# Retention attention and an ELU block on one core: no tensor operation on GpSimd, the decay of the state merged into its sum, one written plan for all steps

## The chip, the cores and the metric

The kernel runs on one core of one Trainium2 chip. The metric is the device time in microseconds of one execution, the median of several runs. The core has five engines with an instruction stream of their own: TensorE (PE, matmuls; PEld are its weight loads), VectorE (DVE), ScalarE (ACT), GpSimd (POOL) and SyncE (SP). Each runs its instructions in order and waits for others by semaphores. SP, ACT and POOL also issue DMAs.

## The reference

The inputs are `q`, `k`, `v` of shape (4, 8, 768, 64): 4 batches, 8 heads, 768 positions, 64 columns; a decay `lam` per head; and two weight matrices, 512 x 2048 and 2048 x 512. Attention goes through each sequence in 12 blocks of 64 positions and carries a 64 x 64 state per head:

```python
for b in range(nb):
    intra = (qb @ kb.T * Dmask) @ vb              # Dmask: lam ** (i - j) for i >= j, else 0
    inter = (qb * lam_pow) @ kv_state             # lam_pow: lam ** (i + 1)
    out[:, :, sl] = intra + inter
    kv_state = lam ** 64 * kv_state + (kb * rev_pow).T @ vb
h = x @ w_in                                      # x: out, as 3072 tokens x 512
g = where(h > 0, h, exp(min(h, 0)) - 1)
return g @ w_out
```

## The kernel before

The work is cut into 24 **steps**. A step is one block of 64 positions of two batches with all heads, 128 tokens; even steps belong to batches 0 and 1, odd ones to 2 and 3, so step s continues the state of step s - 2. Two steps make a **group** of 256 tokens for the ELU block. There are 12 groups.

Attention of a step s, with the names that the plan's words use:

- Loads (`lk`, `lq`, `lv`; line 79): keys, queries and values by GpSimd's DMA queue, cast to 16 bits on the way, twelve buffers each. `w` loads half a quarter of w_in into `wi` (line 100), `y` a quarter of w_out into `wo` (line 111). Step 0's keys and queries come raw by SP and ACT and are cast by `Fk`, `Fq` (line 181).
- Transposes of keys and queries: for s < 10 on TensorE, copied out of PSUM by `C` (`att_C`, lines 239 to 245); from step 10 on by DMA on SP's queue (`T`, `dma_T`, line 256), into two buffers.
- A visit `Aso.us.ss.sx` of TensorE (`visit`) does, for four steps at once: the products of keys and queries of step ss (line 352), the new state product of step us (line 344), the two output products of step so (328 with the old state and the decayed queries, 337 with the masked scores and the values), and the transposes of step sx. `I` begins the first of the output products ahead.
- `P` masks the scores (line 228), `V` decays the values (`vd`, line 193), `Q` decays the queries (`qs`, line 220, two buffers), `D` and `d` decay the old state (`sd`, line 211 on VectorE or GpSimd, line 206 on ScalarE), `N` adds it to the new product in PSUM and writes the state (line 281; for the first two steps a copy, line 285), `X` copies the output to `xt`, the block's input (line 269).

The ELU block: `H` and `h` are units of matmuls with w_in (line 428, 1024 result columns of 128 rows in 8 or 16 matmuls) into one of two PSUM buffers `psH`. `E` and `e` compute exp and relu on ScalarE (lines 438 and 440, or 472 and 474 for the later groups), `G` and `g` join them on VectorE (line 445 or 475). In the first form PSUM is free once ScalarE has read it, in the second when `g` is done. The first six steps go through w_out by `M` (line 495), the output copied by `Z` (502). From group 3 on the product with w_out is done in Strassen's manner, by seven products `p` of eight matmuls each (line 551) over half-size sums `s` (line 533, of `g`) and `B` (line 521, of the weights); `k` keeps a part of PSUM in SBUF (line 581), `a` and `c` add parts to the output tile (lines 585 and 589, four output buffers), `o` stores it (line 570). `K` are constants.

The order of each engine's instructions is the order in which the program emits them. For the first groups it is written out as a string of words, `start`; its beginning is

```python
"Fq K0 Fk V0 A...0 C0 A.0.. K1 A..0. P0 A...1 N0 C1 A0... X0 V1 A..1. P1 A.1.. A1... X1 "
"N1 D2 H0.0.1.0 D3 E0.0.1.0 A...2 V2 C2 Q2 H0.1.1.0 A.2.2. I2 R P2 E0.1.1.0 A2... "
"G0.0.1.0 H0.0.2.4 X2 N2 H1.0.1.0 E0.0.2.4 D4 G0.1.1.0 A...3 G0.0.2.4 E1.0.1.0 C3 V3 "
"H1.0.1.4 Q3 E1.0.1.4 H0.0.2.6 A.3.3. I3 P3 G1.0.1.0 E0.0.2.6 H0.0.2.10 A3... E0.0.2.10 "
```

The early loads are emitted ahead of it: v0, k1, q1, v1, both halves of w0, k2, q2, v2, both halves of w1, k3, q3, v3; `R` emits the later ones. From group 3 on a loop over groups and their eight units `u` emits the rest. Each group there has eight units, eight joins, seven products, four sums, and two of each attention step. In it `decay_q` is on GpSimd for steps 12 and 14 and from 15 to 23, and on VectorE else; `decay_s` is on VectorE up to step 10, on ScalarE for 11 to 13, on GpSimd from 14 to 21.

Of the kernel before, what the change touches and what calls it, by code (L numbers as in the profile page):

```python
# [16 lines left out]
def kernel(  # L17
# [41 lines left out]

    NB = 12  # L60
# [23 lines left out]
    def load_step(s):  # L84
        load("k", s)
        load("q", s)
        load("v", s)

# [8 lines left out]
    def load_wi(i, halves=range(2)):  # L97

        for c in halves:
            ins = nc.gpsimd.dma_start(  # L100
                out=wi[i][half(c)],
                in_=moe_w_in[c * DM // 2 : (c + 1) * DM // 2, i * WB : (i + 1) * WB].rearrange(
                    "(g p) f -> p g f", p=64
                ),
            )
            if (i, c) == (2, 1):

                ins.wait_op(crossed, 1, "sem-ge")

    def load_wo(i):  # L110
        nc.gpsimd.dma_start(
            out=wo[i][:],
            in_=moe_w_out[i * WB : (i + 1) * WB, :].rearrange("(g p) f -> p g f", p=128),
        )

# [14 lines left out]
    load("v", 0)  # L130
    load_step(1)
    load_wi(0)
    load_step(2)
    load_wi(1)
    load_step(3)
    load_wi(2, [0])

# [95 lines left out]
    def att_C(s):  # L233
        if s >= NT:
            return
        T = asb.tile([128, 2, NHP, 2, L], FP16, tag="T", bufs=4, name=f"T{s}")
        psT = st[s].pop("psT")
        if s < NQ:
            nc.vector.tensor_copy(T[:, 0].rearrange("p j r t -> p (j r t)"), psT[0])
            nc.scalar.copy(  # L240
                out=T[:, 1].rearrange("p j r (t g) -> p (j r t) g", g=8),
                in_=psT[1].rearrange("p (g x) -> p x g", g=8),
            )
        else:
            nc.vector.tensor_copy(
                T[:].rearrange("p i j r t -> p r (i j) t"),
                psT.rearrange("p r (x t) -> p r x t", t=L),
            )
        st[s]["T"] = T
# [12 lines left out]
    def att_X(s, eng):  # L262
# [5 lines left out]
        if eng is nc.scalar:  # L268
            nc.scalar.copy(out=to, in_=O)
        else:  # L270
            eng.tensor_copy(to, O)

    def att_N(s):
# [6 lines left out]
        if c:  # L280
            nc.vector.tensor_tensor(
                out=to, in0=psU, in1=st[s]["sd"][:].rearrange("p y j d -> p y (j d)"), op=ALU.add
            )
        else:
            nc.vector.tensor_copy(to, psU)
# [149 lines left out]
    def mm1_e(grp, c0, nc_, n0):  # L435
# [4 lines left out]
        nc.scalar.activation(r[:], psH[:], AF.Relu)  # L440
# [22 lines left out]
    def elu(grp, u):  # L463

        psH, nb, T, name = unit[grp, 0, 2, u]
        if grp == 3 or grp == 4 and u < 6:
            mm1_e(grp, 0, 2, u)
            mm1_g(grp, 0, 2, u, NF2)
            return

        r = msb.tile([128, nb, T], FP32, tag="r", bufs=4, name=f"r{name}")
        nc.scalar.activation(r[:], psH[:], AF.Relu, scale=-1.0)  # L472
        e = msb.tile([128, nb, T], FP32, tag="e", bufs=4, name=f"e{name}")
        nc.scalar.activation(e[:], r[:], AF.Exp, scale=-1.0)  # L474
# [6 lines left out]
    nacc = [0]  # L481
# [8 lines left out]
    def mm2(s, n0):  # L490
        if n0 == 0:
            acc[s] = M[nacc[0] % 2][:]
            nacc[0] += 1
# [6 lines left out]
    def mm2_o(s):  # L500
        o = msb.tile([128, DM], FP32, tag="o", bufs=4, name=f"o{s}")
        nc.scalar.copy(out=o[:], in_=acc.pop(s))
# [56 lines left out]
    def part(grp, i):  # L559
        d = res.setdefault(grp, dict(A=M[0], B=M[1]))  # L560
        lo, hi = slice(0, HD), slice(HD, DM)
# [6 lines left out]
    def store(s, o, cols, queues=(nc.sync, nc.sync)):  # L568
        for r in range(2):
            queues[r].dma_start(out=rows(s, r)[:, cols], in_=o[half(r), cols])  # L570
# [7 lines left out]
    def keep(grp, tag, src, bufs=2):  # L578

        t = res[grp][tag] = msb.tile([128, *src.shape[1:]], FP32, tag=tag, bufs=bufs, name=f"{tag}_{grp}")  # L580
        nc.scalar.copy(out=t[:], in_=src)
# [5 lines left out]
    def c2(grp, queues=(nc.sync, nc.sync)):  # L587
# [5 lines left out]
        store(2 * grp + 1, d[1], slice(0, DM), queues)  # L593
# [12 lines left out]
    def later_loads():  # L606
        load_wi(2, [1])
        load_wo(0)
        load_wi(3)
        load_wo(1)  # L610
        load_wo(2)
        load("k", 4)
        load("q", 4)
        load_wo(3)
        load("v", 4)
        load_step(5)
        load_step(6)
        load_step(7)
        load_step(8)
        load("k", 9)  # L620
        load("q", 9)
        load("k", 10)
        load("q", 10)
        load("v", 9)
        load("k", 11)
        load("q", 11)
        load("v", 10)

    start = (
# [14 lines left out]
    )  # L646
    steps = {
        "I": lambda s: visit(s, None, None, None, True), "C": att_C, "P": att_P, "X": lambda s: att_X(s, nc.scalar),
        "Y": lambda s: att_X(s, nc.vector), "N": att_N, "D": lambda s: decay_s(s, eng=nc.vector), "L": load_step,
        "V": lambda s: decay_v(s, nc.vector if s < 99 else nc.gpsimd),  # L650
        "Q": lambda s: decay_q(s, nc.vector if s < 10 else nc.gpsimd),
        "H": mm1_h, "E": mm1_e, "G": mm1_g, "M": mm2, "Z": mm2_o, "K": consts, "B": w_sum, "T": dma_T,
    }
    for word in start.split():
        if word[0] == "A":
            visit(*(int(x) if x else None for x in word[1:].split(".")))
        elif word[0] == "R":
            later_loads()
        elif word[0] == "F":
            cast0(word[1])  # L660
        else:
            steps[word[0]](*(int(x) for x in word[1:].split(".") if x))

    lo, hi = slice(0, HD), slice(HD, DM)

    five = [(3, 2), (3, 4), (3, 6), (4, 0)]
    nload = 12
    for grp in range(3, NG):  # L670
        old, new = grp - 2, grp - 1
        for u in range(8):
            mm1_h(grp, 0, 2, u, NF2)
            s = 2 * grp + 2 + u // 4
            if s < NS and u % 4 == 0:

                if nload < NS:
                    load("k", nload)
                    load("q", nload)
                if nload <= NS:  # L680
                    load("v", nload - 1)
                    nload += 1
            if s < NS and u % 4 == 1:
                if s not in (10, 12):
                    decay_q(s + 1, nc.vector if s < 10 else nc.gpsimd)
                if s not in (10, 11, 12):
                    decay_s(s + 1, eng=nc.vector if s < 10 else nc.gpsimd)
                visit(
                    s, s if s < NS - NPR else None, s + 1 if s + 1 < NS else None,
                    s + 2 if s + 2 < NT else None,  # L690
                )
                dma_T(s + 3)

            if (grp, u) in five:
                mm2(5, 4 * five.index((grp, u)))
            end = grp == NG - 1
            if old >= 3 and u in (0, 2):
                part(old, {0: 3, 2: 7}[u])
            if new >= 3:
                at_u = {1: 2, 3: 4, 4: 1, 5: 5, 6: 6, 7: 3} if end else {3: 2, 4: 1, 5: 4, 6: 5, 7: 6}  # L700
                if u in at_u:
                    part(new, at_u[u])

            if old >= 3 and u == 1:
                add(old, 0, hi, res[old]["A"][:, hi], "p35")
                store(2 * old, res[old][0], slice(0, DM), ((nc.gpsimd if end else nc.sync),) * 2)
            if old >= 3 and u == 0:
                g_sum(old, 3)
            if new >= 3 and u in (4, 5, 6):
# [101 lines left out]
```

## Time and profile before

| | before |
|---|---|
| median of 3 runs | 205.23 us (204.94 to 205.42) |
| span of the profiled execution | 204.2 us |
| TensorE busy | 189.6 us, 93% |
| VectorE busy | 168.7 us, 83% |
| ScalarE busy | 146.5 us, 72% |
| GpSimd busy | 123.4 us, 60% (with its DMA issues) |

The profiled execution's own time outside the profiler is not listed; its span lies 1.03 us below the median. The span runs from the first to the last instruction. Groups in the profile read: line, engine, operation, written tile, read tiles, partitions x elements, count, then busy time and mean duration, then idle time before them and what ended it.

### The profile page before, as it was taken

The numbers are of one execution on the slowest core, as the hardware profiler recorded it, in microseconds if no ns is written. First come the engines' busy times: TensorE is split into PE (matmuls) and PEld (weight loads), VectorE is DVE, ScalarE is ACT, GpSimd is POOL, SyncE is SP. The second block draws the span as 40 slices with busy tenths as digits, with TensorE's granted clock in tenths as the row PEclk, the third lists the DMA queues.
The fourth block names the chain that finished last, engine by engine and source line by source line (L and its number), as shares of the span: only waits on it lengthen the run. The fifth ranks groups of instructions, "written<-read, shape, count | busy, mean of one in ns | idle before, by whom it ended". The sixth has DMA issues, their size and how long they took to land.

```text
span 204.2 us, 7590 instructions
## 1 busy us (share of the span) xinstructions
PE 189.6 (93%) x3216; PEld 156.6 (77%) x3216; DVE 168.7 (83%) x279; ACT 146.5 (72%) x283; POOL 123.4 (60%) x174
## 2 busy tenths in 40 slices
PE   0679899999999999999999989999999999999991
PEld 0457777647777777888888878888888888888881
DVE  4776996489989998999989999989979866758672
ACT  5626987635774879999878677788688788876820
POOL 8977832598998959997709999999222200020000
PEclk9999999999999999999999999999999999999998
DMA  6999999999999999999999999999915404004043
GB/s 102 157 171 171 152 206 196 180 124 156 117 148 150 173 108 172 153 134 78 74 163 109 206 105 86 185 111 105 169 27 69 94 0 108 0 6 100 3 103 103
DMA packets 94194, 24.36 MB, mean 119 GB/s; under 512 B 86160, under 2 KB 91152, under 8 KB 94160
## 3 DMA queue, kind: packets, MB, share of 16 engines
q0 software_dynamic: 73744, 13.64, 94.7%
q1 hardware_dynamic: 19968, 9.77, 26.9%
q10 hardware_dynamic: 448, 0.46, 1.0%
q8 instruction: 25, 0.41, 0.9%
q14 instruction: 9, 0.07, 0.1%
HBM read 27.27 MB, written 6.29 MB: 164 GB/s over the span
## 4 chain that ended last, share of the span: by engine, by line
PE 85%; DVE 4%; DMA 3%; POOL 3%; issue 2%; ACT 1%; POOLq 0%; DVEq 0%
PE psH L428 40%; PE psM L551 23%; PE psM L495 10%; DMA wi<-in_moe_w_in_dram 3%; PE psO_None L328 2%; POOL vn L79 1%; PE psZ L352 1%; PE psO_None L337 1%; PE psHB L551 1%; PE psHA L551 1%; DVE s L533 1%; PE psZ L344 1%; DVE g L475 1%; POOL kn L79 1%; PE psO L359 1%
## 5 line engine op out<-in xcount | busy, mean ns | idle before, releaser
L428 PE MATMUL psH<-xt,wi 128*128 128x256 f16 (+1 forms) x896 | 100.1, 261 | 1.9 <-ACT e L438 0.6
L428 PEld LDWEIGHTS <-wi 128*128 128x128 f16 x896 | 78.2, 100 | 13.3 <-issue 2.1
L475 DVE SCALAR_TENSOR_TENSOR g<-e,psH 128x512 f16<-128x512 f32 x58 | 39.6, 683 | 14.3 <-ACT e L474 13.8
L472 ACT ACTIVATE r<-psH 128x512 f32<-128x512 f32 x58 | 34.7, 598 | 18.3 <-PE psH L428 18.2
L474 ACT ACTIVATE e<-r 128x512 f32<-128x512 f32 x58 | 36.5, 630 | 1.8
L79 POOL DMA_DIRECT2D kn<-in_k_dram x46 | 32.2, 720 | 9.2 <-DMA wo<-in_moe_w_out_dram 5.1
L79 POOL DMA_DIRECT2D vn<-in_v_dram x48 | 34.1, 741 | 2.0 <-DMA wi<-in_moe_w_in_dram 1.1
L438 ACT ACTIVATE e<-psH 128x512 f32<-128x512 f32 x38 | 22.8, 601 | 14.7 <-PE psH L428 14.4
L551 PEld LDWEIGHTS <-s 128*128 128x128 f16 x288 | 28.1, 98 | 3.3
L445 DVE SCALAR_TENSOR_TENSOR g<-e,r 128x512 f16<-128x512 f32 x38 | 25.7, 685 | 4.1 <-ACT r L440 4.0
L220 POOL TENSOR_TENSOR qs<-TD,powi 128x512 f16<-128x512 f16 x11 | 13.9, 1264 | 19.3 <-PE psO_None L328 13.1
L79 POOL DMA_DIRECT2D qn<-in_q_dram x36 | 25.3, 735 | 0.0
L551 PE MATMUL psM<-wt,s 128*128 128x256 f16 x192 | 24.9, 273 | 0.0
L495 PE MATMUL psM<-wo,g 128*128 128x512 f16 x96 | 24.0, 379 | 0.0
L440 ACT ACTIVATE r<-psH 128x512 f16<-128x512 f32 x38 | 22.9, 602 | 0.0
L551 PEld LDWEIGHTS <-g 128*128 128x128 f16 x216 | 20.6, 98 | 2.6
L193 DVE TENSOR_TENSOR vd<-vn,rev 128x512 f16<-128x512 f16 x22 | 17.2, 783 | 1.8 <-DMA vn<-in_v_dram 1.7
L228 DVE TENSOR_TENSOR P<-psZ,mask 128x512 f16<-128x512 f32 x24 | 16.4, 684 | 2.0 <-PE psZ L344 1.1
L551 PE MATMUL psM<-wo,g 128*128 128x256 f16 x136 | 17.6, 272 | 0.0
L495 PEld LDWEIGHTS <-g 128*128 128x128 f16 x96 | 8.7, 98 | 7.0
L570 POOL DMA_DIRECT2D out_dram<-o x2 | 1.1, 574 | 21.1 <-DVE o L585 21.1
L533 DVE TENSOR_TENSOR s<-g 128x1024 f16<-128x1024 f16 x18 | 13.8, 764 | 0.0
(85 smaller groups left out, 228.7 us busy)
## 6 DMA issues: line engine op xcount, KB each, us to landing
out_dram<-o SPq DMA_DIRECT2D x43, 128.0 KB, 3.3
vn<-in_v_dram POOLq DMA_DIRECT2D x48, 64.0 KB, 5.0
kn<-in_k_dram POOLq DMA_DIRECT2D x46, 64.0 KB, 4.3
qn<-in_q_dram POOLq DMA_DIRECT2D x36, 64.0 KB, 4.5
wi<-in_moe_w_in_dram POOLq DMA_DIRECT2D x8, 256.0 KB, 8.9
wo<-in_moe_w_out_dram POOLq DMA_DIRECT2D x4, 512.0 KB, 12.6
qn<-in_q_dram POOLq DMA_DIRECT2D x5, 128.0 KB, 5.3
kraw<-in_k_dram SPq DMA_DIRECT2D x2, 128.0 KB, 4.7
```

The lines of the kernel that those rows point to most:

```text
L79: nc.gpsimd.dma_start(out=keep[s][half(r)], in_=src[b + r, :, c * L : (c + 1) * L, :].rearrange("h p d -> p h d"),)
L193: eng.tensor_tensor(out=st[s]["vd"][:], in0=vn[s][:], in1=rev[:].unsqueeze(2).broadcast_to([128, H, D]), op=ALU.mult,)
L228: nc.vector.tensor_tensor(out=d["P"][:].rearrange("p y j t -> p y (j t)"), in0=psS, in1=mask[:].rearrange("p y j t -> p y (j t)"), op=ALU. ...
L428: nc.tensor.matmul(psH[:, i, :], lhsT=wi[n // 4][:, kk, (n % 4) * 128 : (n % 4 + 1) * 128], rhs=xt[grp][:, kk, c0 * 128 : c0 * 128 + T], s ...
L438: nc.scalar.activation(e[:], psH[:], AF.Exp)
L440: nc.scalar.activation(r[:], psH[:], AF.Relu)
L445: nc.vector.scalar_tensor_tensor(out=place(grp, c0, nc_, n0, nb, step), in0=e[:], scalar=-1.0, in1=r[:], op0=ALU.add, op1=ALU.min,)
L472: nc.scalar.activation(r[:], psH[:], AF.Relu, scale=-1.0)
L474: nc.scalar.activation(e[:], r[:], AF.Exp, scale=-1.0)
L475: nc.vector.scalar_tensor_tensor(out=place(grp, 0, 2, u, 2, NF2), in0=e[:], scalar=-1.0, in1=psH[:], op0=ALU.add, op1=ALU.max,)
L495: nc.tensor.matmul(acc[s], lhsT=g_of(s, n), rhs=wo[n // 4][:, n % 4, :], start=(n == 0), stop=(n == NFT - 1),)
L551: nc.tensor.matmul(to, lhsT=lhsT, rhs=rhs, start=start and n == 0, stop=stop and n == NF2 - 1, skip_group_check=True,)
```

## The change

- GpSimd only issues loads and one store. All `Q` are on VectorE.
- `D` and `d` are not used. For steps 2 to 21 `N` is four `scalar_tensor_tensor` instructions, one for each pair of heads, that multiply the old state by its decay and add the new product in PSUM.
- A trailing `.1` on a word moves an operation between ScalarE and VectorE: the relu of `E` and `e`, the copies of `X`, `Z` and `k` go to VectorE, those of `C` to ScalarE (its second digit sends the queries' copy to VectorE).
- One string, `plan`, orders everything from the first load to the last store; the loop is gone. The store order on SP changes with it, and step 18 is stored by GpSimd's queue, as before.
- The wait of the second half of w2 on a semaphore of TensorE goes. The PSUM banks of the first six steps' products are assigned by a tuple.

```diff
+    plan = (
+        "lk1 K1 lq1 K0 Fq Fk lv0 lv1 A...0 C0 A..0. P0 A...1 C1.1.1 A..1. P1 A1... lk2 lq2 w1.1 "
+        "V0 w1.0 A0... lv2 lk3 X1.1 A.0.. w0.1 lq3 w0.0 V1 A...2 C2.1 X0.1 w2.1 lv3 lq4 lk4 w2.0 "
+        "H0.0.2.4 V2 N0 A.1.. N1 H0.0.2.6 A.2.2. w3.0 E0.0.2.6 Q2 I2 A...3 P2 A2... E0.0.2.4.1 "
+        "y0 G0.0.2.4 C3.1.1 Q3 w3.1 H0.0.1.0 E0.0.1.0.1 X2 G0.0.2.6 H1.0.1.0 H0.1.1.0 N2 V3 "
+        "A.3.3. E0.1.1.0 P3 I3 A3... lq5 lk5 y1 y2 G0.0.1.0 E1.0.1.0.1 H1.0.1.8 X3.1 H1.1.1.8 "
...
+        "T14 N10 Z4 h4.0 e4.2 k3.p2 X10 lq16 lv16 lk16 h4.5 P11 p3.1 lk15 lq15 T15 h4.6 e4.0 "
+        "g4.2 V11 s3.4 e4.5 s3.3 A11.11.12. h4.3 g4.5 Q12 e4.6 T16 lv15 p3.4 g4.6 e4.3 g4.0 N11 "
+        "X11 h4.7 e4.7 p3.5 h5.1 g4.3 a3.1 g4.1 p3.6 h5.0 g4.7 P12 A12.12.13. V13 V14 k3.c45 "
+        "e5.1 p3.3 e5.0 X12 k3.p35 h5.2 e5.2 g5.1 p4.2 Q13 g5.0 a3.0 o6.0 p3.7 h5.3 N12 g5.2 P13 "
...
+        "e11.3 s10.2 s10.4 g11.2 c9 p10.1 g11.3 h11.5 e11.4 s10.3 p10.5 g11.4 h11.6 e11.5.1 "
+        "a10.1 e11.6 p10.6 k10.u2 g11.5 k10.c45.1 h11.7 p10.3 p10.7 g11.6 a10.2 e11.7 g11.7 j "
+        "p11.1 s11.1 s11.2 k11.u1 s11.4 c10 o20.0 o17.0 o19.0 o21.0 p11.4 p11.5 p11.6 k11.c45 "
+        "k11.u2 s11.3 p11.2 a11.3 o22.1 p11.7 c11 o23.3 p11.3 a11.2 o22.2 o18.5 "
+    )
...
-        if c:
+        if c and "sd" not in st[s]:
+            for j in range(NHP):
+                nc.vector.scalar_tensor_tensor(
+                    out=state[s][:, :, j, :], in0=state[s - NPR][:, :, j, :], scalar=lamL[:, j : j + 1],
+                    in1=psU[:, :, j * D : (j + 1) * D], op0=ALU.mult, op1=ALU.add,
+                )
+        elif c:
...
-        nc.scalar.activation(r[:], psH[:], AF.Relu)
+        if on_dve:
+            nc.vector.tensor_scalar_max(r[:], psH[:], 0.0)
+        else:
+            nc.scalar.activation(r[:], psH[:], AF.Relu)
...
+        "Q": lambda s, e=0: decay_q(s, by(e)), "H": mm1_h, "E": mm1_e, "G": mm1_g, "M": mm2, "Z": mm2_o,
```

`by(0)` is VectorE; no `Q` or `V` of the plan has the digit that would name GpSimd. Of the plan the beginning, the steps 10 to 13 and the end are shown; between them it goes on in the same way.

More of the change, by code (lines that the diff above doesn't have):

```diff
@@ L95, with load_wi @@
     crossed = tc.alloc_semaphore("crossed")
[L97 to L108, printed above, removed]
+    def load_wi(i, c):
+        nc.gpsimd.dma_start(
+            out=wi[i][half(c)],
+            in_=moe_w_in[c * DM // 2 : (c + 1) * DM // 2, i * WB : (i + 1) * WB].rearrange(
+                "(g p) f -> p g f", p=64
+            ),
+        )
     def load_wo(i):
@@ L267, in att_X @@
         O = st[s].pop("O").rearrange("p r (y t) -> p r y t", y=NHP)
[L268 to L271, printed above, removed]
+        copy(eng, to, O)
     def att_N(s):
@@ L498, in mm2, with mm2_o @@
             )
-    def mm2_o(s):
+    def mm2_o(s, on_dve=0):
         o = msb.tile([128, DM], FP32, tag="o", bufs=4, name=f"o{s}")
-        nc.scalar.copy(out=o[:], in_=acc.pop(s))
+        copy(nc.vector if on_dve else nc.scalar, o[:], acc.pop(s))
         for r in range(2):
@@ L631, with sums @@
-    start = (
[14 rows of a table removed]
-    )
-    steps = {
[L648 to L652, printed above, removed]
+    def sums(grp, i):
+        d = res[grp]
+        if i == 0:
+            add(grp, 0, hi, d["A"][:, hi], "p35")
+        if i == 1:
+            add(grp, 0, lo, d["A"][:, hi], "p2")
+        if i == 2:
+            add(grp, 0, hi, d["B"][:, hi], "u2")
+        if i == 3:
+            add(grp, 0, lo, M[1][:, lo], "u1")
```

248 lines of the change are left out of this document (75 added, 173 removed), and 50 rows, old and new, of tables (plan, start).

## The prediction

> **What bounds the kernel now.** I read the page first, then the waits of TensorE, the chain that ended last, and the busy time of the engines by stage.
>
> ```profile
> span 204.2 us, 7590 instructions
> ...
> PE 189.6 (93%) x3216; PEld 156.6 (77%) x3216; DVE 168.7 (83%) x279; ACT 146.5 (72%) x283; POOL 123.4 (60%) x174
> ...
> PE 85%; DVE 4%; DMA 3%; POOL 3%; issue 2%; ACT 1%; POOLq 0%; DVEq 0%
> ```
>
> TensorE is busy for 189.6 of 204.2 us and makes 85% of the chain. A busy TensorE could still be one that waits inside its matmuls, so the next views ask where it stood still and how fast it ran.
>
> ```profile
> PE psM L398 <- DVE qn L181: 6.5, 1, 6.5
> PE psZ L344 <- DVE P L228: 0.8, 1, 0.8
> PE psH L428 <- ACT e L438: 0.6, 1, 0.6
> PE psH L428 <- DVE g L475: 0.5, 2, 0.3
> ```
> ```profile
> 13.24 1.89 PE psH L428 x16
> ...
> 82.63 0.87 PE psH L428 x8
> 83.51 0.87 PE psM L551 x8
> ...
> 199.24 0.89 PE psHB L551 x8
> ```
>
> Its first instruction waits 6.5 us for the first queries; the other named waits are 0.8 us or less, and the two on VectorE's `g` are 0.5 us together. From then on the chain is one unit of eight matmuls (128x256) behind another, 0.87 us each, until 200.1 us; the last 4 us are the last sum and its stores. Both kernels issue the same matmuls. So the change can only win in the first 25 us, in the small waits behind them, and in the tail; it can lose wherever another engine falls behind.
>
> ```profile
> 79.90:160.30 80.40, 79.87 (x1354) 69.63 (x1354) 74.78 (x117) 66.26 (x127) 58.88 (x74) 1.00 1.43 121
> 110.00:130.00 20.00, 19.47 (x292) 16.84 (x289) 19.67 (x28) 15.15 (x28) 20.00 (x25) 1.00 1.56 140
> ```
>
> Columns: stretch, length, busy time of TensorE, its weight loads, VectorE, ScalarE, GpSimd; clock; DMA. From step 10's visit to step 21's, VectorE is busy 74.78 of 80.40 us (93.0%), and TensorE loses 0.53 us. All 0.53 us are lost in the 20 us where VectorE reaches 98.4%. VectorE is the second bound, and where it fills up, TensorE waits.
>
> **What leaves GpSimd, and what that gives VectorE.**
>
> ```profile
> L220 POOL TENSOR_TENSOR qs<-TD,powi 128x512 f16<-128x512 f16 x11 | 13.9, 1264 | 19.3 <-PE psO_None L328 13.1
> L211 POOL TENSOR_TENSOR sd<-st,lamL 128x512 f32<-128x512 f16 x8 | 9.4, 1174 | 2.3 <-DVE st L281 2.3
> ...
> 119.87 1.23 POOL L220 TENSOR_TENSOR qs<-TD,powi 128x512 f16<-128x512 f16 x1
> 120.08 1.58 DVE L193 TENSOR_TENSOR vd<-vn,rev 128x512 f16<-128x512 f16 x1
> ```
> ```profile
> L193 DVE TENSOR_TENSOR vd<-vn,rev 128x512 f16<-128x512 f16 x8 | 5.5, 685 | 1.8 <-DMA vn<-in_v_dram 1.7
> ...
> L193 DVE TENSOR_TENSOR vd<-vn,rev 128x512 f16<-128x512 f16 x11 | 9.7, 882 | 0.0
> L533 DVE TENSOR_TENSOR s<-g 128x1024 f16<-128x1024 f16 x11 | 9.0, 815 | 0.0
> L533 DVE TENSOR_TENSOR s<-s,g 128x1024 f16<-128x1024 f16 x6 | 4.9, 820 | 0.0
> L533 DVE TENSOR_TENSOR s<-g,s 128x1024 f16<-128x1024 f16 x5 | 4.1, 829 | 0.0
> ```
>
> Nineteen operations leave GpSimd, 23.3 us. While one of them runs, VectorE's operations with two inputs in SBUF stretch: `vd` takes 685 ns in the first 60 us, where GpSimd computes nothing, and 882 ns on average in the stretch above, 1.58 us in the case shown. With 685 ns as the clean time of both groups, the stretch holds 11 x 0.20 = 2.2 us for `vd` and 22 x 0.14 = 3.0 us for `s`: 5.2 us that VectorE gets back. GpSimd itself keeps only loads and one store; no wait of TensorE ends on it, so nothing else is earned there.
>
> **What VectorE gets.**
>
> ```profile
> L281 DVE TENSOR_TENSOR st<-psZ,sd 128x512 f16<-128x512 f32 x20 | 13.6, 681 | 0.0
> L585 DVE TENSOR_TENSOR o<-psM,p 128x256 f32<-128x256 f32 x15 | 6.3, 418 | 0.4
> L589 DVE TENSOR_TENSOR o<-psM,c 128x512 f32<-128x512 f32 x8 | 5.5, 690 | 1.2 <-PE psM L551 1.2
> ...
> 24.90 1.28 DVE L445 SCALAR_TENSOR_TENSOR g<-e,r 128x512 f16<-128x512 f32 x2
> ```
>
> Two 0.68 us operations back to back take 1.28 us, so each costs VectorE about 0.61 us. The merged sum of a step is four instructions of 128 columns in place of one of 512. No row shows that size: 256 columns take 418 ns and 512 take 690, which continues to about 0.28 us for 128. Less the 0.07 us overlap this is 0.2 us a piece; I take 0.9 us a step, between 0.8 (full overlap) and 1.14 (none), 0.28 more than the 0.61 of before; the upper end of all is 418 ns a piece, as if nothing were saved by the smaller size. The Trainium skill ("VectorE: DVE Perf Modes", the section on the fixed extra latency) speaks against such splitting: an instruction pays a fixed cost whatever its size, and small tiles pay it per tile; its section on the DRAIN adds that the next operation does not start before the pipe is empty, so that the count should be kept low. By that a step costs four whole durations, and my sum would be 1 us higher. The pair at 24.90 shows some overlap; no row shows it for small operations.
>
> In the stretch from A10 to A21 the plan has 42 `h` and 36 `p` units, against 44 and 37 now: 3 x 0.873 = 2.6 us less TensorE work, so 77.8 us. VectorE there: 74.78, less 5.2 of contention; three more full operations (nine more decayed queries, three sums `s`, two `g` and one `c` fewer), +1.9; eleven merged sums at +0.28, +3.1; one more small copy, +0.4. That is 74.9 of 77.8 us, 96.3%; with 1.14 us a sum it is 99.6%. So the contention that goes pays for about what comes, per time VectorE is fuller than now. Between the two rows of the window view (93.0% loses 0.66% of the time, 98.4% loses 2.65%) 96.3% reads as 1.9%, or 1.5 us in place of 0.5: **+0.9 us**. A decayed query now stands in VectorE's order and holds up all behind it if its transposes are late.
>
> ```profile
> 85.68 1.20 SPq L256 DMA_TRANSPOSE TD<-kn  x1
> 86.97 2.15 SPq L256 DMA_TRANSPOSE TD<-qn  x1
> ...
> TD<-qn SPq DMA_TRANSPOSE x14, 5.3
> ```
>
> The second transpose of a pair is issued 1.3 us after the first and lands 5.3 us later, 6.6 us in all. In the plan each query from step 12 on has at least 9.9 us of TensorE work between what frees the buffer of its transposes and itself. So this costs nothing; a transpose over 3 us late would show on every engine.
>
> Outside the stretch VectorE also takes relus and copies from ScalarE (eight relus, four casts of `xt`, seven kept parts, two output copies), gives ScalarE six copies of transposes, and drops nine decays of the state. At the end it has room (the decayed state of ScalarE, twelve small operations, goes as well, but ScalarE bounds nothing). At the start it has none, which is the next part.
>
> **The first 26 us.** Here the new order matters most.
>
> ```profile
> 1.41 1.54 POOL L79 DMA_DIRECT2D vn<-in_v_dram  x2 [0.15 <-issue]
> ...
> 9.57 1.40 POOL L79 DMA_DIRECT2D vn<-in_v_dram  x2
> ...
> 12.61 0.69 DVE L285 CAST st<-psZ 128x512 f16<-128x512 f32 x1 [0.53 <-PE psZ L344]
> ...
> 16.16 0.69 DVE L193 TENSOR_TENSOR vd<-vn,rev 128x512 f16<-128x512 f16 x1 [1.66 <-DMA vn<-in_v_dram]
> ...
> 25.98 0.30 PE L337 MATMUL psO_None<-P,vn 64*64 64x64 f16 x16
> ```
>
> Step 2's values are issued at 9.57 us and VectorE's `V2` waits for them until 16.16. The plan puts the same loads ahead of them in another order (k1, q1, v0, v1, k2, q2 and two halves of w_in: twelve instructions, now with w0 and then with w1), so `V2` starts at 16.16 again. Before, the first two state copies `N0` and `N1` are done by then (the second at 12.61), and in the plan they stand behind `V2` in VectorE's order, and the relus of two early units come to VectorE too. From `V2` to `P3` the plan has 13 full operations and one merged sum: 13 x 0.61 + 0.9 = 8.8 us, so `P3` ends at 25.0 without a single gap. TensorE's product for step 3 (`A3...`, now at 25.98) can follow at 25.1; I give 0.7 us for gaps (`G0.0.2.4` waits for an exponential, `C3` for the transposes) and take 25.8. At that point TensorE has done five `H` units, where before it had done seven: 2 x 0.873 = 1.75 us. So it is 1.75 - 0.2 = 1.6 us behind. Then `H1.0.1.8` needs a PSUM buffer that `E1.0.1.0`'s relu frees, on VectorE two operations (1.2 us) behind `P3`, with 0.30 us of TensorE work to cover it: 0.9 us at most, I take 0.7. **The start costs 2.3 us** (0.8 if there are no gaps and no wait for the buffer, 3.1 with a later `P3`). Nothing in the loads takes it back: w1 has the bytes of k2 and q2 ahead of it, and its first unit starts later than w0's at 13.24.
>
> **The tail.**
>
> ```profile
> out_dram<-o SPq DMA_DIRECT2D x43, 128.0 KB, 3.3
> ...
> 194.61 1.75 SPq L570 DMA_DIRECT2D out_dram<-o  x3
> ```
>
> The order of the last eight products is kept. Steps 17 and 19 are stored behind step 20 on SP, four issues of 0.6 us more, which are through before the last sum. Zero, if `c10` gets step 18's output buffer (stored early on GpSimd's queue); if it gets step 17's, it waits 3.3 us of landing, and the sum `s11.3` behind it is some 1.5 us late.
>
> **The sum.** 204.2 + 2.3 + 0.9 = 207.4 us of span; the median of the runs, 205.23, lies 1.03 us above the span, so **208.4 us**. About 0.2% (0.4 us) is what a measurement here can tell from no change.
>
> **Rivals.**
> *VectorE over its limit* (chance 0.17). If a piece of the merged sum costs over 0.28 us with no overlap (the 1.14 us case), the stretch is at 99.6% and loses 3.1%, 1.9 us net; at 418 ns a piece VectorE needs 74.9 + 11 x 0.77 = 83.4 of 77.8 us, and TensorE waits 5.6 us and more. That is 209.4 to 214 us; 212 stands for it. For it: the stretched waits at 110 to 130 us. Against it: `e` has four buffers, which lets VectorE lag. The Trainium skill's rule on small tiles, above, points here.
> *The contention decided* (0.17, the faster side). If the stretched `vd` and `s` are what makes TensorE wait, the 0.53 us go, and if step 2's values land by 14.5 us in the new order, `A3...` comes 1.7 us sooner, at 24.1, and the start is even (1.75 - 1.9): 205.2 - 0.5 - 0.15 = 204.5, and 203.9 if the 0.6 us wait on ScalarE's `e` goes too. The Trainium skill ("SBUF — State Buffer", who interferes with whom) says that a VectorE instruction with two SBUF inputs contends with a GpSimd one that reads SBUF; the trace agrees (685 against 882 ns). It decides only if the early loads come sooner; the equal bytes ahead of them speak against it.
> *The tail waits for a buffer* (0.06): 208.4 + 1.5 = 209.9 us.
> *No difference* (0.05): the start costs 0.8 and the stretch gives back its 0.5: 205.5.
> That GpSimd keeps tensor work is excluded: no word of the plan sends any there.
>
> **The numbers.** Forecast 0.55, then 0.17, 0.17, 0.06, 0.05. Slower by over 0.2%: 0.55 + 0.17 + 0.06 = 0.78; within: 0.05; faster: 0.17. The range of 203.9 to 212.5 us leaves out about half of the first rival and the best of the second; the forecast's own is 206 to 210.5 (0.8 to 3.1 at the start, 0.5 to 2 in the stretch).
>
> **What would show it.** `vd` at 685 ns and `s` at 683 throughout; merged sums near 0.28 us a piece; `V2` at 16.2; `A3...` near 25.8 with two units fewer behind it; VectorE at 96% between steps 10 and 21, with TensorE's waits on `g` there over 1 us.
>
> ```profile
> 46.48 0.32 PE L337 MATMUL psO<-P,vn 64*64 64x64 f16 x16
> ```
>
> I am wrong if step 4's product, now at 46.48 us, comes no later for the TensorE work done by then, or if VectorE has idle time between steps 10 and 21 as it has now.

## The result and the profile after

| | before | after |
|---|---|---|
| median of the runs, us | 205.3 (204.94 to 205.42, 4 runs) | 210.98 (210.93 to 212.27, 4 runs) |
| ratio to before | | 1.0265 [1.0203, 1.0327] |
| span of the profiled execution, us | 204.2 | 210.2 |

The change costs 5.7 us. Every ratio here is taken against runs of the kernel before on the same chip, and it leaves disturbed runs out, so it can differ from the quotient of two medians. The profiled execution of the changed kernel is the longest of its four: its span is 210.2 us, those of the other three are 209.0 to 209.2 us. So what follows accounts for about 1 us more than they lost.

The page of the changed kernel first: its span, the busy time of the engines, the shares of the chain that ended last.

```profile
span 210.2 us, 7617 instructions
...
PE 190.8 (91%) x3216; PEld 156.5 (74%) x3216; DVE 180.8 (86%) x356; ACT 138.6 (66%) x256; POOL 101.0 (48%) x155
...
PE 84%; DVE 5%; POOL 4%; DMA 3%; issue 1%; ACT 1%; DVEq 0%; POOLq 0%
```

TensorE does the same 3216 matmuls in nearly the same busy time (190.8 against 189.6 us). So the loss is nearly all idle time, and the question is where it lies. Now the windows of both kernels, cut at the same words of the plan: the first matmul of `A3...`, that of step 4's product, and step 10's visit. First before, then after, which goes on to step 21's visit. Columns: stretch, length, busy time of TensorE, its weight loads, VectorE, ScalarE, GpSimd; clock; DMA.

```profile
0.00:26.00 26.00, 16.28 (x380) 13.57 (x384) 18.31 (x39) 14.94 (x36) 21.01 (x37) 1.00 1.32 152
26.00:46.50 20.50, 20.20 (x278) 13.40 (x278) 15.03 (x26) 13.27 (x25) 11.22 (x17) 1.00 1.42 176
46.50:79.60 33.10, 33.10 (x797) 24.75 (x787) 31.90 (x53) 23.57 (x45) 29.63 (x45) 1.00 1.94 144
```
```profile
0.00:28.25 28.25, 15.44 (x354) 11.65 (x354) 18.12 (x40) 11.81 (x29) 23.28 (x41) 1.00 1.36 156
28.25:48.90 20.65, 19.38 (x279) 14.09 (x281) 16.23 (x29) 12.17 (x23) 12.69 (x20) 1.00 1.48 157
48.90:86.10 37.20, 35.99 (x803) 25.91 (x790) 34.62 (x71) 25.96 (x48) 32.48 (x49) 1.00 1.79 133
86.30:163.50 77.20, 77.20 (x1349) 67.40 (x1338) 75.61 (x155) 60.69 (x110) 31.27 (x46) 1.00 1.32 117
```

TensorE's idle time, length less busy time, is 9.72, 0.30 and 0.00 us before, and 12.81, 1.27 and 1.21 us after. In the stretch from step 10 to step 21 it lost 0.53 us before and loses none now.

- Up to `A3...` it is 3.1 us more idle. It has also done two units less (1.75 us at 0.87 us each), and its busy time is only 0.84 us shorter: the other 0.9 us are work at a slower pace. Together **4.0 us**. Of the idle time 0.7 us come at once: the plan puts `K0`, a product of the mask, ahead of `Fq` on VectorE, and TensorE's first matmul starts at 7.17 us in place of 6.49.
- From there to step 4's product: **1.0 us** more. By step 4's product TensorE has done 24 units of the ELU block, 27 before.
- From there to step 10: **1.2 us** more.
- Steps 10 to 21: **0.5 us** less. The tail is as long as before.

That is 5.7 of the 6.0 us between the two spans; 0.3 us of small differences are not placed. 5 of the 6 us are lost before 49 us.

TensorE's waits after, longest first (engine, tile, line, releaser; total, times, longest):

```profile
PE psM L448 <- DVE qn L221: 7.2, 1, 7.2
PE psO_None L387 <- DVE P L268: 1.2, 2, 0.8
PE psH L478 <- ACT xt L275: 1.2, 1, 1.2
PE psO_None L387 <- DVE xt L277: 0.8, 1, 0.8
PE psH L478 <- DVE r L491: 0.8, 1, 0.8
PE psO L409 <- issue: 0.8, 1, 0.8
```

No wait on a join `g` of VectorE is among them; the prediction had expected over 1 us of those. In their place stand waits of the first 38 us, and a stop ("issue") for which the view has no releaser. The start is best seen in VectorE's timeline after, from `V2` on (start, duration, engine, line, operation; in brackets the idle time before it and what ended it):

```profile
16.26 0.69 DVE L233 TENSOR_TENSOR vd<-vn,rev 128x512 f16<-128x512 f16 x1 [1.56 <-DMA vn<-in_v_dram]
...
18.08 0.69 DVE L335 CAST st<-psZ 128x512 f16<-128x512 f32 x1 [0.53 <-PE psZ L394]
18.69 0.68 DVE L260 TENSOR_TENSOR qs<-T,powi 128x512 f16<-128x512 f16 x1
20.48 0.69 DVE L268 TENSOR_TENSOR P<-psZ,mask 128x512 f16<-128x512 f32 x1 [1.11 <-PE psZ L394]
21.50 0.69 DVE L491 TENSOR_SCALAR r<-psH 128x512 f16<-128x512 f32 x1 [0.33 <-ACT e L488]
...
25.36 1.12 DVE L326 SCALAR_TENSOR_TENSOR st<-st,lamL,psZ 128x128 f16<-128x128 f16 x4
26.39 0.69 DVE L233 TENSOR_TENSOR vd<-vn,rev 128x512 f16<-128x512 f16 x1
27.50 0.69 DVE L268 TENSOR_TENSOR P<-psZ,mask 128x512 f16<-128x512 f32 x1 [0.42 <-PE psZ L394]
```

`V2` starts at 16.26 us, where the prediction put it (16.16). `P3` ends at 28.19 instead of 25.7, and four idle times of VectorE make up 2.4 us on the way. TensorE's timeline says what they wait for; first after, then, before, step 2's scores and VectorE's `P2` and `P3`:

```profile
15.40 1.86 PE L478 MATMUL psH<-xt,wi 128*128 128x256 f16 x8
17.60 0.43 PE L394 MATMUL psZ<-vd,kn 64*64 64x64 f16 x16 [0.34 <-DVE st L335]
17.96 1.89 PE L478 MATMUL psH<-xt,wi 128*128 128x256 f16 x8
19.78 0.43 PE L402 MATMUL psZ<-T 64*64 64x64 f16 x16
...
24.12 1.95 PE L478 MATMUL psH<-xt,wi 128*128 128x128 f16 x32 [1.16 <-ACT xt L275]
...
30.04 1.05 PE L478 MATMUL psH<-xt,wi 128*128 128x128 f16 x16 [0.48 <-DVE xt L277]
...
37.27 1.03 PE L478 MATMUL psH<-xt,wi 128*128 128x256 f16 x8 [0.79 <-DVE r L491]
```
```profile
17.87 0.38 PE L352 MATMUL psZ<-T 64*64 64x64 f16 x16
...
18.45 0.69 DVE L228 TENSOR_TENSOR P<-psZ,mask 128x512 f16<-128x512 f32 x1 [0.67 <-PE psZ L344]
...
24.30 0.69 DVE L228 TENSOR_TENSOR P<-psZ,mask 128x512 f16<-128x512 f32 x1 [0.42 <-PE psZ L344]
```

The first two units take 1.86 and 1.89 us each. At 24.12 two units take 1.95 us together. Two slow units stand ahead of step 2's scores in both kernels. But the first starts at 15.40 here, at 13.24 before; and the second stands here behind step 1's state product, which waits for `N0`'s copy (0.34 us), and `N0` stands behind `V2`. So step 2's scores start at 19.78 instead of 17.87, and VectorE waits 1.11 us at `P2`. The 0.53 us at `N1` are no unit's: they are the way from `N0`'s copy through TensorE's product and back, and before `N1` waits 0.53 us as well. Before, the slow time of TensorE ended near 17.9 us, here near 21.5; e12 below has the same start as the changed kernel and shows what this is worth. The waits at 30.04 and 37.27 are those for `X3` and for the relu of `E1.0.1.4`, both now on VectorE; together they are the idle time of the second stretch.

The groups of the operations that the change moves (count, busy time, mean ns):

```profile
L326 DVE SCALAR_TENSOR_TENSOR st<-st,lamL,psZ 128x128 f16<-128x128 f16 x80 | 22.3, 342 | 1.1 <-PE psZ L394 1.1
L233 DVE TENSOR_TENSOR vd<-vn,rev 128x512 f16<-128x512 f16 x22 | 14.9, 685 | 1.6 <-DMA vn<-in_v_dram 1.6
L596 DVE TENSOR_TENSOR s<-g 128x1024 f16<-128x1024 f16 x18 | 12.3, 685 | 0.1
L260 DVE TENSOR_TENSOR qs<-TD,powi 128x512 f16<-128x512 f16 x14 | 9.5, 685 | 0.0
```

`vd`, `s` and `qs` all take 685 ns: the stretching is gone. A piece of the merged sum is listed with 342 ns, but the pieces overlap: the next operation starts 1.03 us after the first piece (25.36 to 26.39).

### The profile page after: what moved, and what is told of

Its sections match the earlier page's. It is cut to its first block, busy times and chain, and to the rows that moved or that the text cites. A ratio compares the mean times of both kernels' runs of the same rounds, so it can differ in the third digit from the quotient of the medians.

```text
span 210.2 us, 7617 instructions
## 1 busy us (share of the span) xinstructions
PE 190.8 (91%) x3216; PEld 156.5 (74%) x3216; DVE 180.8 (86%) x356; ACT 138.6 (66%) x256; POOL 101.0 (48%) x155
## 4 chain that ended last, share of the span: by engine, by line
PE 84%; DVE 5%; POOL 4%; DMA 3%; issue 1%; ACT 1%; DVEq 0%; POOLq 0%
PE psH L478 39%; PE psM L614 24%; PE psM L558 10%; DMA vn<-in_v_dram 3%; PE psO_None L378 2%; POOL vn L131 2%; PE psZ L394 1%; POOL kn L131 1%; PE psHB L614 1%; PE psHA L614 1%; DVE r L491 1%; DVE g L498 1%; PE psO_None L387 1%; PE psZ L402 1%; PE psO L409 1%
## 5 line engine op out<-in xcount | busy, mean ns | idle before, releaser
L478 PEld LDWEIGHTS <-wi 128*128 128x128 f16 x896 | 76.7, 98 | 15.0 <-issue 3.7
L529 ACT ACTIVATE r<-psH 128x512 f32<-128x512 f32 x56 | 33.4, 597 | 20.7 <-PE psH L478 20.5
L131 POOL DMA_DIRECT2D vn<-in_v_dram x48 | 33.6, 729 | 9.4 <-DMA wo<-in_moe_w_out_dram 6.7
L498 DVE SCALAR_TENSOR_TENSOR g<-e,r 128x512 f16<-128x512 f32 x38 | 25.1, 686 | 2.1 <-ACT r L493 2.0
L558 PE MATMUL psM<-wo,g 128*128 128x512 f16 x96 | 23.4, 379 | 0.0
L326 DVE SCALAR_TENSOR_TENSOR st<-st,lamL,psZ 128x128 f16<-128x128 f16 x80 | 22.3, 342 | 1.1 <-PE psZ L394 1.1
L493 ACT ACTIVATE r<-psH 128x512 f16<-128x512 f32 x32 | 19.2, 601 | 0.0
L233 DVE TENSOR_TENSOR vd<-vn,rev 128x512 f16<-128x512 f16 x22 | 14.9, 685 | 1.6 <-DMA vn<-in_v_dram 1.6
L596 DVE TENSOR_TENSOR s<-g 128x1024 f16<-128x1024 f16 x18 | 12.3, 685 | 0.1
```

Source lines behind the costliest of these rows:

```text
L131: nc.gpsimd.dma_start(out=keep[s][half(r)], in_=src[b + r, :, c * L : (c + 1) * L, :].rearrange("h p d -> p h d"),)
L326: nc.vector.scalar_tensor_tensor(out=state[s][:, :, j, :], in0=state[s - NPR][:, :, j, :], scalar=lamL[:, j : j + 1], in1=psU[:, :, j * D ...
L478: nc.tensor.matmul(psH[:, i, :], lhsT=wi[n // 4][:, kk, (n % 4) * 128 : (n % 4 + 1) * 128], rhs=xt[grp][:, kk, c0 * 128 : c0 * 128 + T], s ...
L498: nc.vector.scalar_tensor_tensor(out=place(grp, c0, nc_, n0, nb, step), in0=e[:], scalar=-1.0, in1=r[:], op0=ALU.add, op1=ALU.min,)
L558: nc.tensor.matmul(acc[s], lhsT=g_of(s, n), rhs=wo[n // 4][:, n % 4, :], start=(n == 0), stop=(n == NFT - 1),)
```

## The experiments

Each kernel is described by its edit of the plan's words. The first question is where in the order the time is lost.

**The two orders crossed (e1, e2).** The seam is visit `A4.4.5.6`, which both orders have. e1 takes the first part from before, e2 from after.

```diff
# e1
-        "lk1 K1 lq1 K0 Fq Fk lv0 lv1 A...0 ... M1.12 A4.4.5.6 "   (the order of after)
+        "lv0 lk1 lq1 lv1 w0.0 w0.1 ... Fq K0 Fk V0 A...0 ... A4.4.5.6 "   (the order of before, D2 to D5 with it)
# e2
         "lk1 K1 lq1 K0 Fq Fk lv0 lv1 A...0 ... M1.12 A4.4.5.6 "
-        "lq7 Z1.1 M2.0 lq11 ... "
+        "lv6 lq7 lv7 ... D4.0 D5.0 G1.1.1.0 ... "   (the order of before, decays and GpSimd's queries with it)
```

> The order of the kernel before up to step 4's visit (with its decays D2 to D5 and its early loads), and from there the order of the changed kernel with merged sums and all queries on VectorE. Theory 'start' (the loss is made in VectorE's order of the first 28 us, up to step 4's visit at most 5 us, and nothing is lost behind it): about 205.5 us, TensorE at step 4's visit near 46.5 us. Rival 'load' (merged sums and queries make VectorE too full everywhere): still about 209 to 211 us, with TensorE waiting on VectorE behind step 4.

> The reverse: the changed kernel's order up to step 4's visit, and from there the order of the kernel before, with the decays of the state apart and the later queries on GpSimd. Theory 'start': 210 to 211 us, as the changed kernel, step 4's visit near 49 us. Rival 'load': about 206 us, as most of the merged sums and all moved queries are undone.

e1: 208.28 us, ratio 1.0103 [1.0067, 1.0139], between the two expectations. e2: 211.79 us, 1.0274 [1.0222, 1.0325], which is the whole loss of the change, as theory 'start' has it. Exchanging the start alone gives back 1.6 of the 2.7%, and the start alone costs as much as everything. Of what e1 still loses, 0.73 us are a wait at the seam and 1.1 us two stops of 0.36 and 0.78 us without a releaser. From step 10 to step 21 it loses nothing:

```profile
81.30:158.30 77.00, 77.00 (x1341) 67.21 (x1330) 75.38 (x155) 60.50 (x110) 34.14 (x51) 1.00 1.38 123
```

**The moved work without the new order (e3, e10, e11).** All three keep the order of before throughout. e10 only moves the queries, e11 only merges the sums, e3 does both.

```diff
# e10: every Q on VectorE
-... d11.0.4 h4.5 Q12.1 A11.11.12. ...   (.1: on GpSimd)
+... d11.0.4 h4.5 Q12 A11.11.12. ...
# e11: merged sums
-... Q9 D9.0 A8.8.9. ... g4.4 d11.0.4 h4.5 ...
+... Q9 A8.8.9. ... g4.4 h4.5 ...
# e3: both
```

> The order of the kernel before throughout, but no tensor operation on GpSimd: all decayed queries on VectorE, and every decay of the state merged into its sum. Theory 'start': the work moved costs little by itself, 205 to 207 us, since 5.2 us of stretched operations go while 11 x 0.61 us of queries and 20 x 0.42 us of merged sums less 9 x 0.61 us of decays come. Rival 'load': 208 us or more, TensorE waits on g of over 2 us in all.

> The kernel before with one edit: the eleven queries of GpSimd on VectorE, all else in its order. VectorE gets 11 x 0.61 = 6.7 us, and loses the part of the 5.2 us of stretching that the queries on GpSimd caused. If VectorE's queue is what loses time in the old order: 206 to 207.5 us, TensorE's waits on g over 1 us. If moved work is hidden: 205.3 us.

> The kernel before with the other edit alone: every decay of the state merged into its sum (20 x 4 pieces), queries as before on GpSimd. VectorE gets 20 x 0.42 us, loses nine decays of 0.61, and the start loses D2 to D5 (step 4's visit near 45.2 us as in the third run). Theory: a gain of 1.3 us at the start and a loss of 1 to 2 us behind it, 205 to 206.5 us. Rival 'merge': over 207 us.

e10: 206.37 us, 1.0022 [0.998, 1.0064]. e11: 206.11 us, 1.0032 [0.9995, 1.007]. Neither can be told from no change. e3: 208.44 and 209.54 us in the two runs that its ratio counts, 1.0135 [1.0052, 1.0217]. That is the time that rival 'load' named, though the waits on joins stay below its 2 us. Windows of e10, e11 and e3 from step 10 to step 21:

```profile
79.50:160.00 80.50, 80.50 (x1359) 69.28 (x1357) 76.73 (x128) 66.67 (x129) 44.75 (x62) 1.00 1.38 121
```
```profile
79.00:159.00 80.00, 79.59 (x1346) 68.49 (x1345) 74.92 (x148) 62.82 (x115) 51.64 (x66) 1.00 1.40 121
```
```profile
78.00:158.00 80.00, 78.43 (x1331) 66.72 (x1317) 75.81 (x155) 62.01 (x113) 37.88 (x56) 1.00 1.30 118
```

VectorE is 95.3, 93.7 and 94.8% busy; TensorE loses 0.00, 0.41 and 1.57 us. So the fill of VectorE does not tell what TensorE loses: e10 is fuller than e3 and loses nothing, and the changed kernel is at 97.9% (75.61 of 77.20 us) and loses nothing. In e3 the waits, over the whole span, are small ones on joins and on a query:

```profile
PE psH L476 <- DVE g L537: 1.6, 5, 0.3
PE psO_None L376 <- DVE qs L258: 0.9, 2, 0.7
```

A possible reason: in the order of before the eight units of a group come at fixed places and a merged sum or a query stands ahead of a join that is just due; the order of after spreads the same work so that a late join meets a TensorE that has something else to do. The four traces agree with it; the places were not varied one by one, so it is argued and not shown. In e3 step 4's product comes at 45.15 us, 1.3 us sooner than before. That is no gain from the decays that are gone: e11 has the same start and is at 46.38 us (45.2 had been expected), and e10, with the decays and the start of before, is at 45.53.

**The merging undone in the new order (e4), and the queries given back (e12).**

```diff
# e4: ahead of each N2 to N21 a decay of its own, on VectorE; N adds it
-... H0.1.1.0 N2 V3 ...
+... H0.1.1.0 D2.0 N2 V3 ...
# e12: Q13 to Q23 on GpSimd again
-... p4.2 Q13 g5.0 ...
+... p4.2 Q13.1 g5.0 ...
```

> The changed kernel with the decay of the state as an operation of its own on VectorE right ahead of each sum, for steps 2 to 21: 0.68 + 0.68 us in place of four pieces of 0.28 us, VectorE about 20 x 0.2 = 4 us fuller. Theory 'start': 211 to 213 us, a fraction of the 4 us lost where VectorE is full and about 0.2 us of it in the start. Rival 'merge' (the split sum with its scalar operand is what costs): faster than the changed kernel, 208 us.

> The changed kernel with the queries of steps 13 to 23 back on GpSimd, in the changed order. VectorE loses 11 x 0.61 = 6.7 us and gets stretched vd and s back. Theory 'start' (the middle loses nothing with all of them on VectorE): no gain, 210.5 to 211.5 us, and TensorE without a wait on VectorE between steps 10 and 21 in either. Rival 'load': 208 to 209 us.

e4: 214.64 us, 1.0414 [1.0365, 1.0464], more than was expected; by the two ratios it is 1.5%, some 3 us, behind the changed kernel. So once all decays are on VectorE, merging them pays. In the order of before, where the decays are spread over three engines, no difference can be told (e11). e12: 211.28 us, 1.0296 [1.0212, 1.038], no better than the change. Its window from step 10 to 21, and its groups of `vd` and `s`:

```profile
85.50:162.50 77.00, 76.62 (x1323) 66.59 (x1322) 71.40 (x144) 60.06 (x109) 42.27 (x55) 1.00 1.18 113
```
```profile
L231 DVE TENSOR_TENSOR vd<-vn,rev 128x512 f16<-128x512 f16 x22 | 14.9, 682 | 1.7 <-DMA vn<-in_v_dram 1.7
...
L594 DVE TENSOR_TENSOR s<-g,s 128x1024 f16<-128x1024 f16 x9 | 7.0, 774 | 0.1
```

VectorE falls to 92.7% and is stretched again in places (774 against 685 ns), and TensorE gains nothing by the one nor loses more than 0.4 us by the other, in small waits on VectorE where none had been expected. VectorE's load in the middle doesn't decide the time of this order.

**What in the start costs the time (e5, e6, e7, e9).** e5 puts the first two state copies ahead of the first unit; e6 puts the relus and copies that VectorE took over in the start back, and with them the copies of transposes that ScalarE took; e7 does both; e9 is e7 with step 2's scores ahead of the second unit.

```diff
# e5 (and e7, e9)
-... w2.0 H0.0.2.4 V2 N0 A.1.. N1 H0.0.2.6 ...
+... w2.0 N0 A.1.. N1 H0.0.2.4 V2 H0.0.2.6 ...
# e6 (and e7, e9)
-... X1.1 ... C2.1 X0.1 ... E0.0.2.4.1 ... C3.1.1 ... E0.0.1.0.1 ... E1.0.1.0.1 ... X3.1 ...
+... X1 ... C2 X0 ... E0.0.2.4 ... C3 ... E0.0.1.0 ... E1.0.1.0 ... X3 ...
# e9, on top of e7
-... H0.0.2.4 V2 H0.0.2.6 A.2.2. w3.0 E0.0.2.6 Q2 I2 A...3 P2 A2... ... X2 G0.0.2.6 ...
+... H0.0.2.4 V2 A.2.2. Q2 I2 P2 H0.0.2.6 w3.0 E0.0.2.6 A2... X2 A...3 ... G0.0.2.6 ...
```

> The changed kernel with the state copies N0 and N1, and the state product of step 1 between them, ahead of the first H unit and of V2. They then fill VectorE's 1.6 us wait for step 2's values. If the order of N0 and N1 behind V2 is what makes the start late: 1.2 us faster than the changed kernel, about 209.5 us, P3 at 26.3 us in place of 27.5. If TensorE's two slow units ahead of step 2's scores (15.4 to 19.8 us) set P2, and so P3: under 0.4 us.

> The changed kernel with every operation that its plan moves between VectorE and ScalarE ahead of step 4's visit put back (the relus of E, the copies of X to ScalarE; C1 to C5 as in the kernel before). If VectorE's length in the start is the cause: 2 to 3 us faster, about 208 to 209 us, with TensorE's waits on r L491 and on xt on VectorE gone. If the chain is set by loads and slow units: under 1 us.

> Both edits of the two runs before it. If they act on the same VectorE chain and it is the cause: 3 to 4 us faster than the changed kernel, 207 to 208 us. If each was hidden behind slow units: no more than 1.5 us.

> The third edit of the start on top of the seventh run: step 2's scores, queries and mask ahead of the second H unit (H0.0.2.6), and its output product and the copy X2 ahead of step 3's transposes and of E0.0.1.0. If TensorE's slow units in front of step 2 and X2 late on ScalarE are the larger part of the start (X2 held H1.0.1.0 back by 1.65 us in the seventh run): step 4's visit 1.5 to 2.5 us earlier than there, 45 to 46 us, and 209 to 209.5 us in all. If the loads (w0, lands near 20.6 us) set it: under 0.7 us.

| | `A3...` | step 4's product | time, us | ratio |
|---|---|---|---|---|
| after | 28.25 | 48.91 | 210.98 | 1.0265 [1.0203, 1.0327] |
| e5 | 28.01 | 48.68 | 211.11 | 1.0279 [1.0168, 1.039] |
| e6 | 27.54 | 47.88 | 211.91 | 1.0297 [1.0184, 1.0411] |
| e7 | 27.15 | 47.48 | 211.59 | 1.0292 [1.0198, 1.0385] |
| e9 | 28.52 | 50.07 | 212.49 | 1.0339 [1.0268, 1.0411] |

How far can one execution be trusted here? Three kernels have the start of the changed one, word for word: after, e2 and e12 reach `A3...` at 28.25, 28.30 and 27.48 us. Three have the start of before: before, e1 and e10 are there at 25.98, 25.70 and 25.09. So e5's 28.01 and e6's 27.54 are no finding, and e7's 27.15 is 0.3 us outside the spread. From `A3...` to step 4's product the times are steadier: 20.66 or 20.67 us in after, e2, e5 and e12, and 20.34 and 20.33 in e6 and e7. There the work moved to VectorE costs 0.3 us. None of this is seen in the time, and what it is lost to behind step 4 stays open.

The three executions of the same start also try the slow units. In e12 TensorE's slow time ended earlier, and the second unit runs at 1.05 us in place of 1.89:

```profile
18.04 1.05 PE L476 MATMUL psH<-xt,wi 128*128 128x256 f16 x8
```

VectorE's idle time at `P2` is gone there, and still `A3...` comes only 0.8 us sooner. Against the same place of before, e1 and e10 it is 1.5 to 2.4 us late, with two units fewer done. So the slow second unit makes some 0.8 of the 4.0 us, and before's second unit was slow as well; most of the start's loss is there without it.

In e7 VectorE is relieved and ScalarE becomes the late one: TensorE's timeline has

```profile
24.02 1.95 PE L476 MATMUL psH<-xt,wi 128*128 128x128 f16 x32 [1.65 <-ACT xt L273]
```

since step 2's input stands behind seven operations of ScalarE. e9 was to take that wait away and missed: its step 4 comes 2.6 us later than e7's. Its windows show a part of the reason:

```profile
24.00:28.00 4.00, 2.43 (x75) 2.02 (x72) 3.57 (x10) 2.86 (x6) 3.67 (x6) 1.00 1.26 176
28.00:32.00 4.00, 3.62 (x58) 3.27 (x54) 2.17 (x4) 1.81 (x4) 1.65 (x3) 0.64 1.39 199
32.00:36.00 4.00, 4.00 (x60) 3.37 (x60) 2.50 (x5) 3.23 (x7) 2.06 (x4) 0.93 1.34 200
```

The granted clock fell to 0.64 from 28 to 32 us, behind four us in which TensorE was busy for 2.43. The Trainium skill ("TensorE: Matmul & The Clock Gate", the section on what is happening) sets the clock by how busy TensorE has been of late, and has a half clock after an idle window of about 3.4 us; here TensorE was only thinly busy, not idle that long, and the clock fell all the same. e7 and the changed kernel keep 1.00 there. The thin stretch alone is not shown to be the cause: e7 has one as thin (TensorE busy for 2.37 us from 20 to 24 us) without a fall. Nor is the fall all of e9's miss: three of its four runs have a mean clock of 0.987 to 0.991, and the fourth, with 0.998 as in the other kernels, took 211.98 us.

**The start of before under the rest of after (e8).** e3's start, without decays, up to `M0.12`, then the order of after: the best pieces by the runs so far.

```diff
-        "lk1 K1 lq1 K0 Fq Fk lv0 lv1 A...0 ... M0.12 V4 ... A4.4.5.6 "
+        "lv0 lk1 lq1 lv1 w0.0 w0.1 ... X1 N1 H0.0.1.0 E0.0.1.0 A...2 ... M0.12 ... A4.4.5.6 "
```

> The old order of the start without its apart decays (as in the third run, where step 4's visit came at 45.2 us in place of 46.5) up to the unit M0.12, then the changed kernel's order with merged sums and all queries on VectorE. The third run lost 3.1 us behind step 4, the changed kernel none. Theory 'start': TensorE ends 1 to 1.5 us earlier than in the kernel before, 204 to 205 us, unless TensorE stops again for 0.8 us near step 7's visit (then 205 to 206). Rival 'load': 207 us or more.

206.89 us, 1.0061 [1.0025, 1.0098]: 4 us better than the change, but behind before, and more than was expected. Step 4's product is at 44.34 us with three units fewer behind it (2.6 us), so 0.5 us behind before. The lead that the expectation took from e3 is, as said, no property of this start. Of these two waits of TensorE the first is at the seam, the second is a stop without a releaser:

```profile
PE psO L376 <- ACT T L273: 1.2, 1, 1.2
PE psO L407 <- issue: 1.1, 1, 1.1
```

**The stops without a releaser.** No kernel was made for them, and only e8's expectation allows for one; all 14 profiled executions together suggest what they are. Windows from the first instruction to the end of the stop, for after (two stops), e2 and e1:

```profile
0.00:69.20 69.20, 54.38 (x1114) 39.89 (x1114) 53.34 (x107) 37.10 (x74) 55.03 (x87) 1.00 1.46 151
0.00:76.77 76.77, 61.49 (x1242) 44.73 (x1242) 59.83 (x121) 42.23 (x83) 59.80 (x94) 1.00 1.56 149
```
```profile
0.00:70.62 70.62, 54.69 (x1114) 39.74 (x1115) 56.00 (x104) 35.97 (x75) 55.03 (x87) 1.00 1.48 149
```
```profile
0.00:64.81 64.81, 53.74 (x1114) 40.12 (x1115) 48.43 (x92) 41.09 (x82) 50.93 (x81) 1.00 1.48 157
```

The times differ by 6 us, the orders differ, and the count of matmuls is 1114 each time, in e4 to e8 as well; the second stop, which e6 has too, comes 128 matmuls and 128 weight loads later. e1 and e11 have one more, smaller stop much earlier, both behind the 349th matmul, at 24.42 us in e1 and here in e11:

```profile
23.89 0.22 PE L392 MATMUL psZ<-vd,kn 64*64 64x64 f16 x3 [0.27 <-issue]
```

So TensorE stops not at a step of the program but at a place in its instruction stream. The page lists a DMA queue for instructions:

```profile
q8 instruction: 25, 0.41, 0.8%
```

These are 25 packets of 16 KB. The Trainium skill ("Advanced Engine Details and Errata", the section on the ISA cache) gives 256 instructions for a 16 KB line; the distance of the two late stops agrees. 25 such packets would be 6400 instructions, close to TensorE's 6432 matmuls and weight loads. In the DMA records the packet ahead of the 1114th matmul begins 1.5 to 2.3 us after TensorE has passed the 986th in the six kernels without a stop there (before 1.82) and 2.4 to 3.5 us in the eight with one (after 2.83). At the ten stops at these two places TensorE goes on 1.30 to 1.62 us after the packet has landed, at the two early ones 1.31 and 1.47 us; of the 18 passages of these two places without a stop four are 1.41 to 1.52 us behind the landing, the others more. So TensorE seems to wait for its next instructions. This is read from the records, not tried, and why the packet comes late stays open. The profiled execution of the changed kernel loses 1.2 us in this way, that of before nothing; whether the three shorter runs of the changed kernel stop too is not recorded.

## Why the prediction was right, and where not

The sign came out, and the place. The size did so in part: 3.2 us forecast, 5.7 measured; 210.98 lies in the stated range (203.9 to 212.5) but above the forecast's own (206 to 210.5). That it is no further off is partly luck: the start was priced too low and a wait for instructions was not foreseen, but the stretch was priced too high. By its steps:

- **The start, +2.3 us forecast, about 5 measured.** The place was right, and `V2` is where it was put. The step that failed is "I give 0.7 us for gaps", with the "13 x 0.61 + 0.9" ahead of it: from `V2` to the end of `P3` 9.5 us were forecast and 11.9 measured. The listed gaps are 2.4 us; of the other 9.5 us 0.7 are work above the 8.8 that were summed. 0.61 us is what an operation costs right behind another; behind a wait it costs its whole 0.69. Three of the four gaps are hand-overs to TensorE and back (`N1`, `P2`, `P3`), which the prediction did not count, though the kernel before has 1.09 us of them in the same stretch (0.67 at `P2`, 0.42 at `P3`). In e12, without the slow second unit, the gaps are still 1.4 us and the whole is 11.0. The prediction also names the later first unit and gives it no price; it starts 2.2 us later. e1 and e2 show the place. That the hand-overs, the later first unit and step 2's input behind ScalarE's exponentials are the reason is argued from the timelines; e5 to e7 and e9, which were to part them, brought no time back.
- **`H1.0.1.8` waits 0.7 us for a relu on VectorE:** not there. `H1.0.1.8` follows `A3...` without a wait. The wait that was meant came later and for another relu: `H0.0.2.10` stands 0.79 us for that of `E1.0.1.4`. That the size agrees is chance.
- **The stretch, +0.9 us forecast, -0.5 measured.** VectorE was to be 96.3% busy and is 97.9%; the reading of TensorE's loss off that share was wrong. It took two windows of one order for a law, and a gain was measured where a loss was forecast. e10, e3 and the changed kernel show that the share alone does not decide it.
- **The merged sum, 0.9 us a step forecast:** 1.03 in the case shown, inside the bounds (0.8 to 1.14). By the Trainium skill ("VectorE: DVE Perf Modes", the section on the DRAIN) the next operation does not start before the pipe is empty; four pieces would then take 4 x 0.342 = 1.37 us. The same section adds, and the prediction left out, that an operation that nothing holds starts earlier. Here the pieces overlap by 0.08 us each, which fits the second. With the decays on VectorE and not merged the kernel would be some 3 us slower still (e4).
- **The contention that goes:** right in size (685 ns), and no use of it is seen in the time (e12).
- **The tail:** zero, as forecast.
- **Around the span, 1.03 us:** some 0.7 us too little. In the later runs of before the time is 1.75 us above the span of the same execution; the forecast had set a span of one execution against the median of others.
- **Not foreseen:** 1.2 us of stops in the profiled execution, read as waiting for instructions.

Of the rivals, VectorE over its limit gave nearly the measured time (212) by a mechanism that did not occur; contention deciding, the tail's buffer and no difference did not occur either.

## What to carry to other kernels

When a chain of short steps goes back and forth between two engines, count its hand-overs one by one and take their sizes from the trace before the change; gaps in such a chain are not a remainder to be rounded, and an operation behind a gap costs its whole duration. Before a difference of under 1 us between two profiled executions is explained, look for kernels that share the stretch word for word: here they differed by 0.8 to 0.9 us at `A3...`. The busy share of a second engine tells that it is near its bound, not what the first one loses: much the same load cost 1.6 us in one order and nothing in another. A stop without a releaser may be counted in instructions instead of in time.

## What the runs showed of the hardware

- TensorE stopped, by the records for its own instructions, behind the 1114th or the 1242nd matmul for 0.44 to 1.09 us in eight of fourteen profiled executions, and behind the 349th for 0.27 and 0.36 us in two.
- When TensorE's slow start ends varies between executions of one order: a second unit at 18 us ran at 1.89 us in after and at 1.05 in e12. The trace's clock record begins, with full clock, at 21.62 and at 16.95 us there, and between 15.15 us (e3) and 22.33 us (e9) in all fourteen. The windows list a clock of 1.00 ahead of it too: the durations show the slow start, the clock's column does not.
- The granted clock fell to 0.64 over four us (e9) behind four us with TensorE busy for 2.43 of them; it did not fall behind 2.37 of four in e7.
- Four pieces of 128 columns from PSUM, 342 ns each as listed, take 1.03 us in a row.
